# Top-k attention and a PReLU MLP on one core: a hand-written drain with masks on VectorE, and another order on TensorE

## The chip, the cores and the metric

The kernel runs on one core of a Trainium2 chip. The core has five engines that run their own instruction streams: TensorE (PE in the profile; its weight loads are PEld), VectorE (DVE), ScalarE (ACT), GpSimd (POOL) and SyncE (SP, used here to issue DMAs). The metric is the device time of one execution in microseconds (us), and the median over the runs is compared.

## The reference

For 8 batches and 8 heads of 576 tokens with 64 dimensions, attention keeps in each row only the scores that are at least as large as the row's 32nd largest. The heads are then joined to 4608 tokens of 512 columns, which pass an MLP with 2048 hidden units and a leaky activation with a slope for each unit.

```python
scores = (q @ k.transpose(0, 1, 3, 2)) / sqrt(64)
kth    = np.partition(scores, -32, axis=-1)[..., -32:-31]
scores = np.where(scores >= kth, scores, -1e9)
attn   = softmax(scores) @ v                      # 8 x 8 x 576 x 64
x      = attn.transpose(0, 2, 1, 3).reshape(4608, 512)
h      = x @ w_in                                 # 4608 x 2048
g      = np.maximum(h, 0) + alpha * np.minimum(h, 0)
out    = g @ w_out                                # 4608 x 512, float32
```

## The kernel before

**Tiling.** Two heads form a pair `p` (32 pairs, four to a batch). A "duo" is 128 query rows of both heads of one pair (type "n", with the row block `j` from 0 to 3), or the last 64 rows of both heads of two pairs (type "m", the tails). There are `ND` = 144 duos, 18 to a batch. The last batch has its duos ordered by row block, so that each row block becomes a chunk of 128 tokens for the MLP; the batches before it have chunks of 256 tokens, and the tails of two batches share a chunk of 128.

**The life of a duo `d`**, each step in a later slot:
- `st_qk` (TensorE): scores of the duo into one PSUM tile `ps_sc` (pool `ps_s`, one buffer).
- `st_exit` (ScalarE): copy of the scores to `s_sb` in SBUF, 128 x 2 x 576 in float32.
- slot `d` (VectorE, in `dve_slot`): maxima of 8 over six groups of 96 columns for each head; for two duos together `threshold_steps` (`fold`, `negate`, `least`, `turn`) makes from these a first threshold `p9`, which lies near the wanted one.
- slot `d+2`: `st_count` (ScalarE): the sign of (threshold - score) and its sum, so how many scores lie above; `st_y` (GpSimd): score times sign; `row` (VectorE): the 8 largest of that, so the scores next to the threshold.
- slot `2m+4` of a pair of duos: `pick_steps` (VectorE): from the count and these neighbours the exact 32nd largest, kept in `KT` as a multiple of `BIG` = 2^60.
- slot `d+4`: `st_relu` (ScalarE and GpSimd): Relu(KT - BIG * score), which is 0 for the kept scores and huge for the others, is subtracted from the scores.
- slot `d+5`: `st_exp` (ScalarE): Exp of the result to `w` (bfloat16), and a DMA transpose of `w` to `wT`, issued by SP.
- slot `d+7`: `st_av` (TensorE): `wT` times V, whose 65th column is 1 and gives the sum of the row; `norm_a`, `norm_b` (VectorE): reciprocal and product, for two duos together; `st_xT`: a DMA transpose of the finished rows `x` to `xT` on SP.

**The MLP.** When a chunk's `xT` is issued, `mlp_ready` puts its steps into queues: units of h (16 matmuls of 128 columns, or 8 of 256) into `soon`, from which they go to `hq` two slots later, and parts of the output product (one matmul with `w_lin_b` and four with `w_out_b`, four parts for 128 tokens) into `oq`. `h_pe` issues one unit, `h_dve` the Relu of it to `gT` on VectorE, `o_pe` one part, `o_act` the copy of a finished `pz` to `o_sb` on ScalarE, and `o_sp` the store. A part of the next tokens is held back while a finished `pz` has not been copied (`not stores`). The leaky part of the activation is taken out of the sum beforehand: `w_out_b` holds w_out times (1 - alpha), and `w_lin_b` is w_in times (alpha * w_out).

**The order.** All engines' instructions stand in the order in which the program writes them, slot by slot. In a slot `n` the order on TensorE is: one unit of h (or, if there is none, `keep_warm`: four matmuls on zeros, `rest<-idle` in the profile), the transposes that prepare a later pair (`prep`, tile `tps`), the scores of duo `n+1`, the AV of duo `n-7`, one part of the output product, and at the end a second part if more than two are ready, or else `keep_warm`. The tiles of h, of `prep` and of `keep_warm` share two PSUM buffers (`ps_h`). An additional unit of h goes into an even slot when more than 9 units wait (more than 4 from slot 118 on). In the first 17 slots the wide copies of `prep` go to VectorE.

**The end.** The last four duos have shorter lags, and four more slots (144 to 147) run the same loop; for all duos the path is sign, product, maxima, Relu, subtraction, Exp, transpose, AV. Then a loop issues what remains of the MLP.

Of the kernel before, what the change touches and what calls it, by code (L numbers as in the profile page):

```python
# [17 lines left out]
NG = 6  # L18
# [41 lines left out]
def fast_path(tc, q, k, v, moe_w_in, moe_w_out, moe_alpha, out, flag):  # L60
# [27 lines left out]
    with ExitStack() as ctx:  # L88
# [171 lines left out]
        def norm_of(n):  # L260

            m = n - 7 if n < ND + 1 else {ND + 1: ND - 5, ND + 2: ND - 3, ND + 3: ND - 1}.get(n, 0)
            return m if m > 0 and m % 2 else 0
# [49 lines left out]
        def dve_slot(n, f_late):  # L313

            norm = norm_of(n)
            rows = [d for d in duos_at("row", n)]
            picks = [f for m in duos_at("pick", n) for f in pick_steps(m)]
            if on(n):
                s = T["s", n]
                if n % 2 == 0:  # L320
                    T["up", n // 2] = two.tile([128, 4, NG // 2, 8], FP32, name="up", tag="up")
                up = T["up", n // 2]
                for i in range(2):
                    r = 2 * (n % 2) + i
                    for g in range(NG):
                        o = 24 * r + 8 * (g // 2)
                        m = DVE.max(out=(lo if g % 2 else up)[:, r, g // 2, :],
                                    in_=s[:, i, GW * g:GW * g + GW])
                        if g % 2:
                            sm(m, [], [(o, o + 8)])  # L330
                            if picks:
                                picks.pop(0)()
                if n % 2 == 0:
                    h_dve()
                    for d in rows:
                        row(d, 0)
                    if norm:
                        norm_a(norm)
                    for d in rows:
                        row(d, 1)  # L340
                    if norm:
                        norm_b(norm)
                else:
                    fold, negate, least, turn = threshold_steps(n // 2)
                    fold()
                    h_dve()
                    negate()
                    for d in rows:
                        row(d, 0)
                    least()  # L350
                    turn()
                    for d in rows:
                        row(d, 1)
            else:
                if norm:
                    norm_a(norm)
                    norm_b(norm)
                early = picks and duos_at("pick", n)[0] < ND // 2 - 1
                if early:
                    for f in picks:  # L360
                        f()
                if not norm:
                    h_dve()
                for d in rows:
                    row(d, 0)
                    row(d, 1)
                if not early:
                    for f in picks:
                        f()
                if norm:  # L370
                    h_dve()
            if f_late:
                h_pe()
                h_dve()
# [6 lines left out]
        for d in range(ND):  # L381
            last = d - (ND - 4) if d >= ND - 4 else None
            for kind, lag, drain in (("count", 2, (2, 2, 2, 1)), ("relu", 4, (4, 3, 3, 2)),
                                     ("exp", 5, (5, 4, 4, 3)), ("av", 7, (6, 5, 5, 4))):
                at_slot = d + (lag if last is None else drain[last])
                if d < ND - 4:
                    at_slot = min(at_slot, ND + 1)
                stage.setdefault((kind, at_slot), []).append(d)
        for (kind, n), l in list(stage.items()):
            if kind == "count":  # L390
                stage["row", n] = l
        for m in range(ND // 2):
            stage["pick", 2 * m + (4 if m < ND // 2 - 1 else 3)] = [m]
# [28 lines left out]
        def st_exp(n):  # L422
            w = ws[n % 3]
            ACT.activation(w[:, :, 0:S], T.pop(("s", n)), AF.Exp, scale=att_scale)
            wt = three.tile([128, 10, 128], BF16, name="wT", tag="wT")
# [84 lines left out]
        def mlp_ready(xt, rows):  # L510
            ntok = sum(r[1] for r in rows)
            e_n = 512 // ntok
            ch = {"done": 0}
# [15 lines left out]
            for i in range(NFT // e_n):  # L529
                soon.append((now[0] + 2, lambda i=i: unit(i)))  # L530

            def part(t0, a):
                gt = ch["g"]
                if a == 0:
                    ch["z"] = ps_z.tile([128, DMODEL], FP32, name="pz", tag="z")
# [30 lines left out]
        def h_dve():  # L566
            if act:
                ch, f0, e_n, ph = act.pop(0)
                DVE.tensor_scalar(ch["g"][:, f0:f0 + e_n, :], ph, 0.0, None, ALU.max)
# [152 lines left out]
        for n in range(ND + 4):  # L722
            end = n >= ND
# [4 lines left out]
            if end:  # L728
# [349 lines left out]
```

## Time and profile before

| | |
|---|---|
| median of 3 runs | 839.5 us (837.88 to 840.24) |
| the profiled execution | 840.79 us |
| its span, first to last instruction | 839.0 us, mean granted TensorE clock 0.977 |
| busy: TensorE, VectorE, ScalarE, GpSimd | 751.4, 759.2, 763.5, 753.7 us |
| TensorE, warming matmuls (`rest<-idle`) | 62.4 us, 224 matmuls |
| GpSimd's first product `y` and last subtraction | 20.96 us and about 803.4 us |
| last copy of scores begins | 778.7 us |
| last output copy begins | 831.99 us |

A row of the groups names the engine, the operation, the tile written and the tiles read, the shape and the count; then the busy time and the mean time of one in ns, then the idle time of the engine just before these instructions and what ended it. A row of a timeline gives the start, the time, the engine, the operation and, in brackets, the idle time before it. The line of nearly all instructions is that of a helper (`Ordered`, line 32), so that the tile names tell them apart.

### The profile page before, as it was taken

How to read it: one execution, taken by the hardware profiler on the slowest of the kernel's cores; microseconds unless marked ns; L12 is line 12 of the kernel's file. 1: busy time of each engine (PE TensorE's matmuls, PEld its weight loads, DVE VectorE, ACT ScalarE, POOL GpSimd, SP SyncE). 2: the span in 40 equal slices, each digit the busy share in tenths (PEclk: the TensorE clock that was granted, in tenths of full speed). 3: DMA queues.
4: the chain of work that ended last, by engine and by line, in shares of the span. 5: the costliest groups of instructions: out<-in, count | busy, mean ns of one | idle time of the engine just before them, and what ended most of it. 6: DMA issues, size and time to landing. Idle time of an engine off the chain costs nothing.

```text
span 839.0 us, 17803 instructions
## 1 busy us (share of the span) xinstructions
PE 751.4 (90%) x5382; PEld 426.0 (51%) x5382; DVE 759.2 (90%) x3475; ACT 763.5 (91%) x1255; POOL 753.7 (90%) x706
## 2 busy tenths in 40 slices
PE   8878798998989898898989899898989899989696
PEld 5334344555545554455545455555545555456463
DVE  4879977999999999999999999999999999999731
ACT  4789988999999999999999999999999999999820
POOL 1798988999999999999999999999999999999920
PEclk9979899999999999999999999999999999999898
DMA  6599867556656556556656556556666555444441
GB/s 142 157 165 182 157 124 151 92 122 134 118 120 131 109 103 148 107 133 120 128 114 142 112 96 143 107 132 121 131 113 142 120 96 103 88 83 79 81 87 41
DMA packets 344231, 100.19 MB, mean 119 GB/s; under 512 B 338032, under 2 KB 338048, under 8 KB 344128
## 3 DMA queue, kind: packets, MB, share of 16 engines
q1 hardware_dynamic: 341152, 92.13, 55.6%
q0 software_dynamic: 1776, 6.56, 3.2%
q8 instruction: 44, 0.72, 0.3%
q14 instruction: 59, 0.48, 0.2%
q10 hardware_dynamic: 1200, 0.30, 0.2%
HBM read 36.71 MB, written 9.44 MB: 55 GB/s over the span
## 4 chain that ended last, share of the span: by engine, by line
DVE 38%; POOL 19%; ACT 17%; PE 15%; issue 6%; DMA 3%; SPq 0%; ACTq 0%; POOLq 0%
DVE small L32 11%; DVE p L32 10%; POOL y L32 9%; POOL s_sb L32 9%; DVE up L32 7%; DVE gT L32 5%; ACT r L32 5%; ACT sg L32 5%; PE ps_sc L32 4%; ACT s_sb L32 4%; PE pz L32 3%; ACT w L32 3%; PE ph L32 3%; PE rest L32 2%; DMA wT<-w 2%
## 5 line engine op out<-in xcount | busy, mean ns | idle before, releaser
L32 POOL TENSOR_TENSOR y<-s_sb,sg 128x576 f32<-128x576 f32 x288 | 362.1, 1278 | 40.6 <-ACT sg L32 40.0
L32 POOL TENSOR_TENSOR s_sb<-s_sb,r 128x576 f32<-128x576 f32 x288 | 362.3, 1279 | 8.9 <-ACT r L32 8.6
L32 ACT ACTIVATE sg<-s_sb,p 128x576 bf16<-128x576 f32 x288 | 221.4, 773 | 8.0 <-DVE p L32 6.8
L32 DVE MAX8 p<-y 128x8 f32<-128x576 f32 x288 | 215.1, 747 | 8.1 <-POOL y L32 7.6
L32 DVE MAX8 up<-s_sb 128x8 f32<-128x96 f32 x864 | 211.8, 245 | 9.8 <-ACT s_sb L32 9.8
L32 DVE MAX8 small<-s_sb 128x8 f32<-128x96 f32 x864 | 216.1, 250 | 0.0
L32 ACT ACTIVATE r<-s_sb,KZ 128x576 bf16<-128x576 f32 x288 | 206.6, 769 | 0.4 <-DVE KZ L32 0.4
L32 PE MATMUL ps_sc<-qkT 64*128 64x512 f32 (+2 forms) x768 | 184.1, 569 | 18.7 <-ACT s_sb L32 18.6
L32 ACT COPY s_sb<-ps_sc 128x1152 f32<-128x1152 f32 x144 | 159.2, 1105 | 21.8 <-PE ps_sc L32 21.5
L32 ACT ACTIVATE w<-s_sb 128x1152 bf16<-128x1152 f32 x144 | 166.4, 1156 | 5.9 <-POOL s_sb L32 5.8
L32 PE MATMUL ph<-xT,w_in_b 128*128 128x256 bf16 (+1 forms) x1408 | 150.8, 255 | 5.3 <-ACT qkT L32 2.9
L32 PE MATMUL pz<-w_out_b,gT 128*128 128x512 bf16 x576 | 148.8, 381 | 0.3 <-DVE gT L32 0.3
L32 PEld LDWEIGHTS <-w_in_b 128*128 128x128 bf16 x1408 | 119.2, 99 | 48.7 <-issue 12.0
L32 PE MATMUL xo<-v,wT 128*128 128x65 bf16 (+3 forms) x1600 | 127.0, 199 | 11.2 <-DMA wT<-w 11.2
L32 PEld LDWEIGHTS <-wT 128*128 128x128 bf16 (+3 forms) x1600 | 97.9, 100 | 40.3 <-DMA wT<-w 11.8
L32 DVE TENSOR_SCALAR gT<-ph 128x512 bf16<-128x512 f32 x144 | 97.2, 675 | 19.4 <-PE ph L32 19.3
L32 PEld LDWEIGHTS <-gT 128*128 128x128 bf16 x576 | 55.9, 98 | 71.9 <-issue 16.9
L32 PEld LDWEIGHTS ps_sc<-qkT 64*128 64x128 f32 (+1 forms) x768 | 56.0, 170 | 64.4 <-ACT s_sb L32 30.3
L32 PEld LDWEIGHTS ps_sc<-kd,qkT 128*128 128x128 f32 x256 | 38.3, 189 | 97.7 <-issue 95.4
L32 PE MATMUL pz<-w_lin_b,xT 128*128 128x512 bf16 x144 | 55.6, 386 | 16.4 <-ACT o_sb L32 16.3
L32 PE MATMUL rest<-idle 128*128 128x512 bf16 x224 | 62.4, 409 | 8.6 <-DVE gT L32 5.2
L32 PE MATMUL ps_sc<-kd,qkT 128*128 128x128 f32 x256 | 62.8, 327 | 0.0
(57 smaller groups left out, 572.2 us busy)
## 6 DMA issues: line engine op xcount, KB each, us to landing
k_st<-in_k_dram SPq DMA_DIRECT2D x64, 128.0 KB, 2.8
v_st<-in_v_dram SPq DMA_DIRECT2D x64, 128.0 KB, 2.7
q_st<-in_q_dram SPq DMA_DIRECT2D x62, 128.0 KB, 2.8
out_dram<-o_sb SPq DMA_DIRECT2D x31, 256.0 KB, 2.5
w_st<-in_moe_w_out_dram POOLq DMA_DIRECT2D x4, 1024.0 KB, 6.6
wT<-w SPq DMA_TRANSPOSE x144, 3.5
w_in_b<-in_moe_w_in_dram POOLq DMA_DIRECT2D x4, 512.0 KB, 6.5
k_st<-in_k_dram SPq DMA_DIRECT2D x32, 32.0 KB, 2.7
```

The source lines that it names most:

```text
L32: ins = self.tc.keep_in_program_order(f(*a, **kw))
```

## The change

- **Slots 0 to 143.** On TensorE the scores of duo `n+1` and the AV stand first, then h (or `keep_warm`), then `prep`. The AV and the norm of the duos below 13 come a slot later (lag 8). On VectorE the Relu of h (`h_relu`) stands at the end of the slot; the threshold steps, the row maxima and the norm come before it. Units of h may start one slot after their chunk is issued instead of two. An additional unit goes in when more than 7 wait (even slots); from slot 118 on, when more than 3 wait (any slot) or more than 1 (even slots). From slot 118 on the second part of the output product is issued whenever one is ready.
- **First slots.** In slots 0 to 3 the copies of `prep` go to ScalarE.
- **Drain.** The four extra slots are replaced by a list of steps. For duos 140, 142 and 143 (`D-3`, `D-1`, `D`) `st_all` takes the Exp of all scores, before the threshold is known (into the score PSUM tile for even duos, into an SBUF tile for odd ones), and `st_mask` writes (score >= kth) * Exp to `w` on VectorE. Some Relus of h go to ScalarE. `fill(k)` issues k steps of the MLP, a part if one is ready and else a unit of h.
- **Last chunk.** The output product of the last 128 tokens uses a tile of the score pool and is not held back by an uncopied `pz`.

```diff
         def dve_slot(n, f_late):
...
+            turn = None
+            if n % 2:
+                fold, negate, least, turn = threshold_steps(n // 2)
+                fold()
+                negate()
+            for d in rows:
+                row(d, 0)
+            if turn:
+                least()
+                turn()
+            if norm:
+                norm_a(norm)
+            for d in rows:
+                row(d, 1)
+            if norm:
+                norm_b(norm)
+            h_relu()
             if f_late:
                 h_pe()
-                h_dve()
+                h_relu()
...
+            for kind, lag in (("count", 2), ("relu", 4), ("exp", 5), ("av", 8 if d < 13 else 7)):
+                stage.setdefault((kind, d + lag), []).append(d)
...
-                soon.append((now[0] + 2, lambda i=i: unit(i)))
+                soon.append((now[0] + 1, lambda i=i: unit(i)))
...
+                    if ch["last"]:
+                        ch["z"] = ps_s.tile([128, 1536], FP32, name="ps_last", tag="s")[:, 0:DMODEL]
...
-            if ready() and not stores:
+            if ready() and (not stores or oq[0][0]["last"]):
...
-        for n in range(ND + 4):
+        for n in range(ND):
...
-            if not h_pe() and not end:
-                keep_warm()
             wide_copy = n % 2 and (n, "prep") in todo
-            if n > 3:
-                run(n, "prep", 1)
             if n and on(n + 1):
                 st_qk(n + 1)
-            if n < 4:
-                run(n, "prep", 2)
-            if not end:
-                for m in duos_at("av", n):
-                    st_av(m)
-            late = len(hq) > (9 if n < 118 else 4) and n % 2 == 0 or end
+            for m in duos_at("av", n):
+                st_av(m)
+            if not h_pe():
+                keep_warm()
+            run(n, "prep", 2 if n < 4 else 1)
+            near = n > 117
+            late = len(hq) > (1 if near else 7) and (n % 2 == 0 or near and len(hq) > 3)
...
-                if not (end or ready() > 2) or not o_pe():
-                    if not end and not did:
-                        keep_warm()
+            elif not ready() > (0 if near else 2) or not o_pe():
+                if not did:
+                    keep_warm()
...
-                on_dve = short and n > 16 or wide and (n < 17 or n % 2 == 0)
+                on_dve = n > 3 and (short and n > 16 or wide and (n < 17 or n % 2 == 0))
...
+        def picked(m):
+            for f in pick_steps(m):
+                f()
+            kv = T["kv", m] = two.tile([128, 4], FP32, name="kv", tag="kv")
+            DVE.tensor_scalar(kv, KT[:, 4 * m:4 * m + 4], 1.0 / BIG, None, ALU.mult)
+
+        def st_all(d):
+            if d % 2 == 0:
+                e = two_of(ps_s.tile([128, 1536], FP32, name="e_ps", tag="s"), 960, S)
+            else:
+                e = qk_p.tile([128, 2, S], FP32, name="e_sb", tag="qkT")
+            ACT.activation(e, T["s", d], AF.Exp, scale=att_scale)
+            T["e", d] = e
+
+        def st_mask(d):
+            w, e, s_ = ws[d % 3], T.pop(("e", d)), T.pop(("s", d))
+            kv = T["kv", d // 2]
+            for i in range(2):
+                r = 2 * (d % 2) + i
+                DVE.scalar_tensor_tensor(out=w[:, i, 0:S], in0=s_[:, i, :], scalar=kv[:, r:r + 1],
+                                         in1=e[:, i, :], op0=ALU.is_ge, op1=ALU.mult)
+            st_wT(d)
...
+        D = ND - 1
+        now[0] = ND
+        o_sp()
+        st_av(D - 6)
+        h_pe()
+        st_all(D - 3)
+        st_count(D - 1)
+        st_y(D - 1)
+        st_exp(D - 4)
+        st_count(D)
+        st_y(D)
+        o_act()
+        picked(D // 2 - 1)
+        st_mask(D - 3)
+        fill(2)
+        st_av(D - 5)
+        normed(D - 6)
+        row(D - 1, 0)
+        st_relu(D - 2, 0)
+        st_relu(D - 2, 1)
+        row(D - 1, 1)
+        h_relu()
+        now[0] += 1
+        o_act()
+        fill(2)
+        row(D, 0)
+        h_relu(ACT)
+        st_all(D - 1)
+        row(D, 1)
+        picked(D // 2)
+        st_av(D - 4)
+        fill(1)
+        st_mask(D - 1)
+        h_relu(ACT)
+        st_all(D)
+        normed(D - 4)
+        now[0] += 1
+        o_act()
+        o_sp()
+        fill(2)
+        st_mask(D)
+        st_exp(D - 2)
+        st_av(D - 3)
+        fill(1)
+        h_relu(ACT)
+        st_av(D - 2)
+        normed(D - 2)
+        now[0] += 1
+        o_act()
+        o_sp()
+        fill(3)
+        h_relu(ACT)
+        st_av(D - 1)
+        st_av(D)
+        normed(D)
+        fill(2)
+        check_low()
```

After this list a loop issues the rest of the MLP, one part, one Relu of h (VectorE and ScalarE in turn), one output copy and one store in each round.

More of the change, by code (lines that the diff above doesn't have):

```diff
@@ L315, in dve_slot @@
             norm = norm_of(n)
-            rows = [d for d in duos_at("row", n)]
+            rows = duos_at("count", n)
             picks = [f for m in duos_at("pick", n) for f in pick_steps(m)]
[L318 to L333, printed above, removed]
-                    h_dve()
[L335 to L371, printed above, removed]
@@ L512, in mlp_ready @@
             e_n = 512 // ntok
-            ch = {"done": 0}
+            ch = {"done": 0, "last": rows[-1][0] == NTOK - 192}
             pieces = []
@@ new lines, in fast_path @@
+        o_act()
[18 more added lines that the diff above has]
+        check_low()
+        turn = 0
+        while hq or act or soon or oq or stores:
+            now[0] += 1
+            while h_pe(2):
+                pass
+            o_pe()
+            h_relu((DVE, ACT)[turn % 2])
+            turn += 1
+            o_act()
+            o_sp()
+            if not hq and not act:
```

74 lines of the change are left out of this document (38 added, 36 removed).

## The prediction

> **What bounds the kernel now.** I read the busy times of the page first, then the busy time by stage, then the groups, then who waited for whom, and last the timelines of the start and the end and the chain that ended last.
>
> ```profile
> PE 751.4 (90%) x5382; PEld 426.0 (51%) x5382; DVE 759.2 (90%) x3475; ACT 763.5 (91%) x1255; POOL 753.7 (90%) x706
> ```
> ```profile
> core 0 of [0], span 839.0 us
> core 0: us, PE busy (x) PEld busy (x) DVE busy (x) ACT busy (x) POOL busy (x), PEclk, DMA share, GB/s
> 33.00:160.00 127.00, 107.06 (x620) 52.05 (x618) 109.84 (x494) 116.93 (x193) 115.16 (x111) 0.92 0.76 147
> 160.00:646.00 486.00, 447.39 (x3295) 258.04 (x3292) 476.57 (x2218) 480.50 (x787) 478.56 (x434) 1.00 0.61 122
> 646.00:784.00 138.00, 130.21 (x961) 74.60 (x959) 134.04 (x620) 133.39 (x220) 132.48 (x116) 1.00 0.49 96
> 784.00:839.00 55.00, 39.11 (x383) 26.06 (x379) 18.94 (x43) 17.00 (x26) 17.11 (x15) 0.87 0.33 65
> ```
>
> Four engines at 90% is an average. By stage, VectorE, ScalarE and GpSimd stand at 98 to 99% from 160 to 646 us, so reordering buys little there. In 33 to 160 us they lose 10 to 17 us each. From 784 us, when the last score maxima are through, all three are mostly idle and TensorE is busy 39.11 of 55 us. So there are three places to look at: the ramp, the middle, the drain.
>
> ```profile
> L32 POOL TENSOR_TENSOR y<-s_sb,sg 128x576 f32<-128x576 f32 x288 | 362.1, 1278 | 40.6 <-ACT sg L32 40.0
> L32 POOL TENSOR_TENSOR s_sb<-s_sb,r 128x576 f32<-128x576 f32 x288 | 362.3, 1279 | 8.9 <-ACT r L32 8.6
> L32 ACT ACTIVATE sg<-s_sb,p 128x576 bf16<-128x576 f32 x288 | 221.4, 773 | 8.0 <-DVE p L32 6.8
> L32 DVE MAX8 p<-y 128x8 f32<-128x576 f32 x288 | 215.1, 747 | 8.1 <-POOL y L32 7.6
> ...
> L32 DVE TENSOR_SCALAR gT<-ph 128x512 bf16<-128x512 f32 x144 | 97.2, 675 | 19.4 <-PE ph L32 19.3
> ```
>
> GpSimd has four instructions of 1.28 us for each duo, 5.1 us. It needs the sign from ScalarE, which needs the threshold from VectorE, which needs the score copy. A stall anywhere in that ring is read at GpSimd's idle time.
>
> **Start (first copies by ScalarE, scores ahead of the warming matmuls).** The rows are from the timelines of VectorE, TensorE, ScalarE and GpSimd.
>
> ```profile
> 24.19 1.27 DVE L32 COPY qkT<-tps 128x512 f32<-128x512 f32 x2
> ```
> ```profile
> 24.91 3.09 PE L32 MATMUL rest<-idle 128*128 128x512 bf16 x8 [2.39 <-DVE qkT L32]
> ```
> ```profile
> 29.95 1.12 ACT L32 COPY s_sb<-ps_sc 128x1152 f32<-128x1152 f32 x1 [5.62 <-PE ps_sc L32]
> ```
> ```profile
> 32.81 2.52 POOL L32 TENSOR_TENSOR y<-s_sb,sg 128x576 f32<-128x576 f32 x2 [5.11 <-ACT sg L32]
> ```
>
> Read upwards: GpSimd stood 5.11 us for a sign, ScalarE 5.62 us for scores, and TensorE had two groups of warming matmuls (3.09 us) ahead of those scores, which waited 2.39 us for VectorE's copy of a transpose, because both h buffers were full. The change gives those copies to ScalarE, which is idle by then, and puts the scores ahead of the second warming group. The scores come about 2.4 + 3.09/2, or 3.9 us, earlier. ScalarE spends about 1.3 us on two copies ahead of the signs of duo 1, while GpSimd is still at duo 0. I take -3 us; the bounds are 0 (the sign then waits for VectorE) and -4.5.
>
> **Ramp (scores and AV first; AV a slot later for d below 13).** First GpSimd's waits in 33 to 160 us, then rows of TensorE's and ScalarE's timelines.
>
> ```profile
> POOL y L32 <- ACT sg L32: 16.4, 12, 5.1
> ```
> ```profile
> 54.79 1.07 PE L32 MATMUL xo<-v,wT 128*128 128x65 bf16 x10 [3.05 <-DMA wT<-w]
> 55.79 3.60 PE L32 MATMUL rest<-idle 128*128 128x512 bf16 x8
> ```
> ```profile
> 62.17 1.12 ACT L32 COPY s_sb<-ps_sc 128x1152 f32<-128x1152 f32 x1 [3.22 <-PE ps_sc L32]
> ```
>
> The 16.4 us contain the 5.1 of the start, so 11.3 are left. The pattern is in the three rows: an AV waits 3.05 us for its transposed weights, two warming groups follow (3.60 us), and the scores behind them make ScalarE wait 3.22 us. Now the scores stand ahead of AV, of one of the two groups (1.8 us) and of the transposes of the preparation, and AV has one more slot for its transfer. No work is saved; what moves back are h and the preparation, and who waits for those (the relu and the copies, both at the slot's end) does not hold up the ring. VectorE and ScalarE were busy 109.84 and 116.93 of 127 us, so they could give back some 10 us at most. I take about half of 11.3, -5; bounds 0 and -9.
>
> **Middle (relu at the end of VectorE's slot).** GpSimd's waits for the sign in 160 to 784 us, then ScalarE's for the threshold over the whole span.
>
> ```profile
> POOL y L32 <- ACT sg L32: 6.8, 9, 1.9
> ```
> ```profile
> ACT sg L32 <- DVE p L32: 6.8, 12, 1.1
> ```
>
> The threshold of a pair now leaves VectorE one relu (0.675 us) earlier, which covers most of ScalarE's 12 waits for it (0.57 us in the mean). The price is that an h buffer comes free about 1.3 to 2 us later, by the row maxima (0.747 each) and the norm that now precede the relu. TensorE meets that only where a second h or a warming group asks for the buffer in the same slot. I take -3 us, bounds -7 and +4.
>
> **More MLP steps from slot 118.** The warming matmuls in 646 to 784 us, then TensorE by form in 784 to 839 us.
>
> ```profile
> 646.00:784.00 138.00, 8.21 (x32) 1.00 0.49 96
> ```
> ```profile
> L32 PE MATMUL ph<-xT,w_in_b 128*128 128x128 bf16 x237 | 16.6, 228 | 0.0
> L32 PE MATMUL pz<-w_lin_b,xT 128*128 128x512 bf16 x17 | 6.6, 391 | 2.8 <-ACT o_sb L32 2.8
> ```
> At 784 us there remain 237/16, or 15 units of h, and 17 parts of the output product. By the chain of waits:
>
> ```profile
> 803.42 1.17 ACT w L32
> 804.59 0.02 issue
> 804.61 3.76 DMA wT<-w
> ...
> 813.99 1.79 PE ph L32 x32
> 815.77 1.08 PE pz L32 x5
> ...
> 831.99 0.58 ACT o_sb L32
> ```
>
> two units take 1.79 us and one part 1.08. The last three chunks of 128 tokens have to wait for their attention, 12 units and 12 parts; so at most 3 units and 5 parts, 8 us, can go ahead. Room for them is there in 646 to 784 us: 138 - 130.21 = 7.8 us idle and 8.21 of warming. With h a slot earlier, a second h from four waiting units on, and a second part whenever one is ready, I take 6 us as moved. Each unit brings its relu of 0.675 us to a VectorE that is at 97% there: 3 of them cost the ring +2 us. The 6 us count within the drain.
>
> **Drain.** Rows of GpSimd's, TensorE's and SP's timelines, and one stretch by stage.
>
> ```profile
> 790.66 4.98 POOL L32 TENSOR_TENSOR s_sb<-s_sb,r 128x576 f32<-128x576 f32 x4
> ```
> ```profile
> 792.40 1.07 PE L32 MATMUL xo<-v,wT 128*128 128x65 bf16 x10 [5.13 <-DMA wT<-w]
> 793.40 1.89 PE L32 MATMUL ph<-xT,w_in_b 128*128 128x128 bf16 x16
> ```
> ```profile
> 809.92 1.19 SPq L32 DMA_TRANSPOSE xT<-x  x1
> ```
> ```profile
> 790.00:800.00 10.00, 5.53 (x37) 3.67 (x38) 4.01 (x10) 7.11 (x10) 7.23 (x7) 0.50 0.56 107
> ```
>
> For duos 140, 142 and 143 the change drops two relus of ScalarE and two subtractions of GpSimd (1.28 us) each: 6 x 1.28 = 7.7 us leave GpSimd. It puts an Exp of 1.17 us on ScalarE ahead of the threshold, and six masking instructions on VectorE. No row shows that instruction at this size. The nearest are the maximum over 576 elements, 0.747 us, and the relu, 0.675; the far end is GpSimd's two-input form, 1.28; none is free, as 576 elements have to be read. I take 0.72, 4.3 us for six, on a VectorE with 18.94 us of work in 55.
>
> In the new order the mask of 140 is done near 788 us, where its Exp had to wait for two of the subtractions that begin at 790.66. The rows of 143 are done near 792, the masks of 142 and 143 near 794.5 and 796.5, the Exp of 141 near 796.5, since ScalarE has two full Exps, two relus and two output copies before it. Their three weight transposes stand one behind the other on SP's queue, so the last lands near 802 (before: 804.61 + 3.76 = 808.4). AV of 142 and 143 stands behind three MLP steps, so the last x transpose starts near 808 instead of 809.92. Attention ends only some 2 us earlier. The gain lies in TensorE not standing. Before, it did 39.1 us of work in the 47.9 us from 784 to 831.9, and about 2.7 of those were the half clock of 790 to 800 us (a unit of h 1.89 us against 0.9). So 36.4 us were work at full clock and 11.5 lost. After: 36.4 - 6 = 30.4 us of work, and I leave 6.5 lost (waits of AV, of the last x, of the last relu): 36.9 instead of 47.9, -11 us. The last copy and store, 7 us from 831.99 to the end, stay. Bounds: -4 (nothing moved ahead, most of the standing remains) and -16. Where the MLP steps run out, AV's wait of up to 5 us is seen again.
>
> The half clock follows the 5.13 us stand that begins at 787.3. The Trainium skill (TensorE: Matmul & The Clock Gate, "What's actually happening") says that an idle window of about 3.4 us halves the clock and that some 3.4 us of sustained work restore it. The row agrees on the first; on the second it differs, as the half clock lasted 10 us. By the rule, filled gaps mean no half clock.
>
> A rule that speaks against the change: the Trainium skill (SBUF — State Buffer, "Who interferes with whom") has a VectorE instruction with two SBUF inputs and a GpSimd instruction that reads SBUF exclude each other for a whole instruction. The mask of 143 alone has both inputs in SBUF (140 and 142 read the Exp from PSUM). By it the two masks of 143 would each wait for one subtraction of 141, 2.6 us at most, nothing if these are over by 794 as I have them; the sum would be -17.5 at worst instead of -20. No row of this kernel shows the case.
>
> **Sum.** -3 - 5 - 3 + 2 - 11 = -20 us. The profiled execution took 840.8 us (its span 839.0 and 1.8 around it), so it would become 820.8; the median of the runs, 839.5, lies 1.3 below it: 819.5.
>
> **Rivals.** *Only the drain pays.* The ramp's loss is not TensorE's order but three engines at 86 to 92% that wait on each other in turn. For: the middle shows all three full. Against: the scores' waits of 5.62 and 3.22 us have warming matmuls ahead of them. Then 839.5 - 11, about 829.
>
> *The drain changes its wait.* SP's three transposes and the late Exp of 141 leave TensorE standing, and the half clock comes back: the drain gives -4, the rest -9, so 826.5.
>
> *Slower: the late relu holds the h buffer.*
>
> ```profile
> PE rest L32 <- DVE gT L32: 5.2, 10, 0.8
> ```
>
> TensorE already waited 5.2 us for it, ten times. With the buffer free 1.3 to 2 us later, TensorE stands in each slot with a second h, and the next scores stand behind it. Its slack is (7.8 + 8.2) us over the 26 slots of 646 to 784 us, 0.6 a slot; 1.65 - 0.6, about 1 us, in one of four of the 126 slots from 18 on is 31 us, which turns -20 into +11: 850. It decides from 20 us lost, 0.65 us in each such slot. Against: between two score copies ScalarE has two signs (1.55 us) and an Exp (1.17), so scores may be late by over 2 us before anything waits.
>
> *The edits cancel:* copies on ScalarE delay its signs by what the order gains, and the masks take on VectorE what GpSimd saves: 838 to 840.
>
> **How the numbers follow.** Forecast 0.55, only the drain 0.17, a new wait in the drain 0.15, cancel 0.05, slower 0.08. The low end takes the gains at nearly all of their better bounds for start and drain and two thirds for the rest, about -32: 807. Above, the drain's rivals with a little lost in the middle reach 836. A measurement of this kernel tells about 0.3%, 2.5 us, from no change: faster 0.87, same 0.04, slower 0.09.
>
> **What would show it.** Right: GpSimd's 5.11 us wait down to about 2; ScalarE's waits for scores down by half or more; its wait for the threshold mostly gone; under 15 units of h left after the last score maxima; no TensorE gap above 3.4 us and a clock of 1.0 in the drain; some 37 us from there to the last matmul instead of 48. Wrong: longer TensorE waits for gT, less busy vector engines from 160 us on, masks above 1.2 us, or a half clock in the drain.

## The result: slower, 869.9 us against 838.7

The changed kernel takes 869.89 us (median of 4 runs, 868.97 to 877.8) against 838.69 for the kernel before: a ratio of 1.0393, 95% interval 1.0329 to 1.0457. The forecast was 819.5 with a range of 807 to 836. The direction was wrong.

The page of the changed kernel, and its busy time in four stretches (us; then busy time and count of each engine, the granted clock and DMA). The stretches end at about the same slots as those shown of before: slot 24, slot 117, and the end of the score maxima, within two duos.

```profile
span 867.9 us, 17761 instructions
...
PE 761.7 (88%) x5329; PEld 426.9 (49%) x5414; DVE 766.4 (88%) x3472; ACT 768.1 (89%) x1260; POOL 748.3 (86%) x702
```
```profile
core 0: us, PE busy (x) PEld busy (x) DVE busy (x) ACT busy (x) POOL busy (x), PEclk, DMA share, GB/s
33.00:140.00 107.00, 90.33 (x539) 44.61 (x550) 99.50 (x450) 105.41 (x175) 104.36 (x101) 0.95 0.87 166
140.00:657.00 517.00, 463.82 (x3295) 262.16 (x3348) 487.16 (x2233) 484.89 (x790) 480.17 (x434) 0.98 0.58 115
657.00:820.00 163.00, 146.88 (x1052) 82.92 (x1068) 143.69 (x652) 141.64 (x231) 139.40 (x123) 0.98 0.45 88
820.00:868.00 48.00, 32.61 (x309) 21.39 (x310) 16.71 (x36) 15.44 (x26) 10.70 (x11) 0.91 0.35 69
```

GpSimd, ScalarE and VectorE had been at 98 to 99% between the ramp and slot 117. Now they are at 93 to 94%, and in the last batch at 86 to 88%. The work is the same, so the time is waiting; what they waited for is read below. The ramp is better: three engines lost 10 to 17 us there, now they lose 2 to 8.

The clearest measure is when the copy of each duo's scores begins on ScalarE, read from its timeline. How far a kernel is ahead of the kernel before (minus: behind), in us, at duos 24, 117 and 143, and how long it takes from the last copy to the end of its span:

| kernel | median us | at 24 | at 117 | at 143 | then to the end |
|---|---|---|---|---|---|
| before | 838.69 | 0 | 0 | 0 | 60.3 |
| changed | 869.89 | 12.1 | -17.0 | -35.9 | 53.3 |
| e1 Relu early | 874.85 | 8.5 | -23.3 | -42.0 | 52.9 |
| e2 h first | 918.72 | 11.8 | -55.4 | -85.5 | 52.8 |
| e3 both back | 872.25 | 10.3 | -18.8 | -37.6 | 54.9 |
| e4 old step rules | 856.34 | 10.4 | -6.7 | -17.6 | 60.2 |
| e5 both back, old rules | 831.08 | 9.7 | 8.5 | 8.5 | 60.2 |
| e6 Relu early, old rules | 862.27 | 12.2 | -11.3 | -17.0 | 62.2 |
| e7 h first, old rules | 878.04 | 11.6 | -25.1 | -38.0 | 61.1 |
| e8 = e5, h one slot earlier | 841.43 | 11.8 | 10.5 | 5.2 | 63.9 |
| e9 = e5, second h from 7 | 842.53 | 12.2 | 1.9 | -1.2 | 60.6 |
| e10 = e5, more steps from slot 118 | 834.13 | 9.9 | 8.8 | 2.7 | 57.6 |
| e11 = e5, drain in another order | 827.06 | 9.6 | 8.7 | 8.7 | 54.4 |
| e12 = e4, parts ready a slot later | 839.55 | 8.3 | 0.0 | -5.3 | 61.9 |
| e13 = e4, preparation first | 859.36 | 11.7 | -9.8 | -21.5 | 60.5 |
| e14 = e4, both of these | 838.70 | 10.8 | 8.0 | 3.9 | 61.0 |

The profiled execution of e12 took 847.9 us, 8 above its median, so its row of differences is worse than its usual run; that of e8 lies 2 us below its median. Kernels that are alike up to slot 18 differ there by up to 2 us, so smaller differences in the table are not read.

So the changed kernel gains 12 us by slot 24, loses 29 from 24 to 117 and 19 from 117 to 143, and gains 7 behind that: 12.1 - 29.1 - 18.9 + 7.0 = -28.9, the difference of the spans (839.0 and 867.9).

**Start and ramp.** GpSimd's first wait that was 5.11 us, and its waits up to slot 24, which were 11.3 us besides:

```profile
29.49 2.51 POOL L32 TENSOR_TENSOR y<-s_sb,sg 128x576 f32<-128x576 f32 x2 [1.85 <-ACT sg L32]
```
```profile
POOL y L32 <- ACT sg L32: 2.3, 5, 0.8
```

**The middle.** TensorE's timeline in the changed kernel, one slot, and then ScalarE's and VectorE's next instruction that waited for it:

```profile
428.58 1.05 PE L32 MATMUL ph<-xT,w_in_b 128*128 128x256 bf16 x8
429.46 0.38 PE L32 MATMUL pz<-w_lin_b,xT 128*128 128x512 bf16 x1
429.68 0.59 PE L32 MATMUL pz<-w_out_b,gT 128*128 128x512 bf16 x2
432.79 1.03 PE L32 MATMUL pz<-w_out_b,gT 128*128 128x512 bf16 x2 [2.52 <-DVE gT L32]
433.75 2.08 PE L32 MATMUL ps_sc<-qkT 64*128 64x512 f32 x4
```
```profile
436.54 1.12 ACT L32 COPY s_sb<-ps_sc 128x1152 f32<-128x1152 f32 x1 [0.54 <-PE ps_sc L32]
```
```profile
437.10 0.18 DVE L32 RECIPROCAL KZ<-xo 128x4 f32<-128x4 f32 x1 [1.50 <-PE xo L32]
```

The unit of h ends at 429.6. A part of the output product is issued behind it whose last two matmuls need the Relu of that unit. The Relu stands at the end of VectorE's slot and runs at 432.06. TensorE stands 2.52 us in the middle of a part, the next scores and AV stand behind it, and ScalarE and VectorE then wait for those. The stand costs more than its own time: TensorE's granted clock (the third figure from the right) is then halved for 3.41 us, and the four score matmuls take 2.08 us, against 1.13 in the slots before. Two stretches, in the columns of the table above:

```profile
429.39:432.80 3.41, 0.89 (x7) 0.27 (x5) 3.34 (x15) 3.24 (x6) 3.41 (x4) 1.00 0.75 152
432.80:436.21 3.41, 3.41 (x8) 1.07 (x9) 2.81 (x16) 3.20 (x6) 3.41 (x4) 0.50 0.38 78
```

Not every stand is followed by this: the trace of the changed kernel has five such stretches of half clock between slots 24 and 117, that of the kernel before none.

The program allowed the part that stood because `ready()` counts a Relu as done when it is written, not when it has run; while the Relu came early in VectorE's slot, that made no difference. The other pattern is on VectorE, where a second unit of h ends a slot:

```profile
416.18 0.69 DVE L32 TENSOR_SCALAR gT<-ph 128x512 bf16<-128x512 f32 x1 [1.13 <-PE ph L32]
```
```profile
421.41 0.78 ACT L32 ACTIVATE sg<-s_sb,p 128x576 bf16<-128x576 f32 x1 [1.70 <-DVE p L32]
```
```profile
422.36 2.51 POOL L32 TENSOR_TENSOR y<-s_sb,sg 128x576 f32<-128x576 f32 x2 [1.47 <-ACT sg L32]
```

VectorE stands 1.13 us for h and is late with the next threshold, and the wait runs through ScalarE to GpSimd. In 160 to 640 us, GpSimd's waits for the sign, at the end of these chains, and TensorE's waits of parts for the Relu, each before and then after; the last row, of after alone, is a wait of the warming matmuls for ScalarE's copies:

```profile
POOL y L32 <- ACT sg L32: 3.4, 4, 1.9
PE pz L32 <- DVE gT L32: 0.3, 1, 0.3
```
```profile
POOL y L32 <- ACT sg L32: 24.7, 19, 3.2
PE pz L32 <- DVE gT L32: 16.5, 9, 2.9
PE rest L32 <- ACT qkT L32: 8.1, 7, 1.8
```

### The profile page after: what moved, and what is told of

The parts are those of the page before. It is cut to its first block, busy times and chain, and to the rows that moved or that the text cites. A ratio compares the mean times of both kernels' runs of the same rounds, so it can differ in the third digit from the quotient of the medians.

```text
span 867.9 us, 17761 instructions
## 1 busy us (share of the span) xinstructions
PE 761.7 (88%) x5329; PEld 426.9 (49%) x5414; DVE 766.4 (88%) x3472; ACT 768.1 (89%) x1260; POOL 748.3 (86%) x702
## 4 chain that ended last, share of the span: by engine, by line
DVE 40%; PE 30%; POOL 12%; ACT 9%; issue 4%; DMA 3%; SPq 1%; ACTq 0%; POOLq 0%; DVEq 0%
DVE small L32 11%; DVE p L32 10%; PE ps_sc L32 9%; PE pz L32 7%; DVE up L32 7%; PE ph L32 6%; POOL y L32 6%; DVE gT L32 5%; POOL s_sb L32 5%; PE xo L32 5%; ACT sg L32 3%; ACT r L32 2%; ACT s_sb L32 2%; DVE qkT L32 2%; DMA wT<-w 2%
## 5 line engine op out<-in xcount | busy, mean ns | idle before, releaser
L32 POOL TENSOR_TENSOR s_sb<-s_sb,r 128x576 f32<-128x576 f32 x282 | 354.6, 1279 | 14.6 <-ACT r L32 14.3
L32 ACT ACTIVATE sg<-s_sb,p 128x576 bf16<-128x576 f32 x288 | 221.3, 773 | 16.8 <-DVE p L32 16.0
L32 ACT ACTIVATE r<-s_sb,KZ 128x576 bf16<-128x576 f32 x282 | 202.4, 768 | 2.9 <-DVE KZ L32 2.9
L32 PE MATMUL pz<-w_out_b,gT 128*128 128x512 bf16 x539 | 146.7, 388 | 24.4 <-DVE gT L32 20.1
L32 PE MATMUL ph<-xT,w_in_b 128*128 128x256 bf16 (+1 forms) x1408 | 153.7, 257 | 13.7 <-DVE gT L32 7.7
L32 ACT ACTIVATE w<-s_sb 128x1152 bf16<-128x1152 f32 x141 | 162.8, 1155 | 1.8 <-POOL s_sb L32 1.6
L32 PEld LDWEIGHTS <-w_in_b 128*128 128x128 bf16 x1408 | 111.3, 99 | 33.7 <-issue 11.3
L32 DVE TENSOR_SCALAR gT<-ph 128x512 bf16<-128x512 f32 x137 | 92.9, 679 | 26.1 <-PE ph L32 26.0
L32 PEld LDWEIGHTS ps_sc<-qkT 64*128 64x128 f32 (+1 forms) x768 | 53.3, 170 | 117.4 <-ACT s_sb L32 56.4
L32 PEld LDWEIGHTS ps_sc<-kd,qkT 128*128 128x128 f32 x256 | 39.1, 193 | 100.7 <-issue 94.7
L32 PE MATMUL rest<-idle 128*128 128x512 bf16 x234 | 66.5, 394 | 16.1 <-ACT qkT L32 9.6
L32 ACT ACTIVATION_READ_ACCUMULATOR sg<-s_sb,p 128x1 f32 x288 | 55.8, 194 | 0.0
```

The lines of the kernel that those rows point to most:

```text
L32: ins = self.tc.keep_in_program_order(f(*a, **kw))
```

## The experiments

Three theories: RELU, the late Relu; ORDER, h and preparation behind scores and AV; STEPS, the rules for additional MLP steps. Rows of waits below give the sum, the number and the longest, over slots 24 to 117 unless stated.

**e1, e2 and e3: the order and the Relu undone, with the new step rules.**

```diff
# e1, in dve_slot
                 fold()
+                h_relu()
                 negate()
+            else:                # even slots, after the maxima
+                h_relu()
...
                 norm_b(norm)
-            h_relu()
# e2, slots from 24 on
+                if not h_pe():
+                    keep_warm()
+                run(n, "prep", 1)
             if n and on(n + 1):
                 st_qk(n + 1)
             for m in duos_at("av", n):
                 st_av(m)
-            if not h_pe():
-                keep_warm()
-            run(n, "prep", 2 if n < 4 else 1)
# e3: both, from slot 24 on
```

> The changed kernel with one thing undone: the Relu of h stands again where it stood before in VectorE's slot (after the maxima in even slots, after the fold in odd ones). Before and after, the copies of the scores stand apart by -12 us at slot 24 (the changed kernel ahead), +17 at slot 117, +34 at slot 141. Theory RELU (the late Relu makes the parts of the output product wait for gT, with the next scores behind them): most of the 29 us of slots 24 to 117 come back, TensorE's 16.5 us of waits for gT in 160 to 650 us vanish, time 835 to 845. Rival ORDER (h behind scores and AV is what is late; an early Relu then waits on VectorE for h): no gain or a loss, 870 to 900, with VectorE's waits for h at over 60 us.

> The changed kernel with h (or the warming matmuls) and the preparation ahead of scores and AV again from slot 24 on; the Relu of h stays at the slot's end. ORDER: the 29 us of slots 24 to 117 come back, 840 or less. RELU: the parts still wait for the Relu at the slot's end; at most a third comes back, 860 or more. STEPS (more units and parts overfill TensorE): no change, about 870.

> The changed kernel with both undone from slot 24 on: Relu early and h first; start, ramp, additional MLP steps and drain stay as changed. If RELU and ORDER together hold the loss of slots 24 to 117: 12 us ahead at slot 24, still 10 to 12 ahead at slot 117. If the additional steps cost nothing themselves, the drain's 6 us come on top: about 820. STEPS as the cause of the 17 us of slots 118 to 143: 835 to 840.

874.85, 918.72 and 872.25 us (ratios 1.044, 1.0961 and 1.0399; intervals 1.0416 to 1.0464, 1.0935 to 1.0986, 1.0375 to 1.0424). None recovers anything. e1 came out as ORDER had it, e2 against it and 49 us above the changed kernel, which no theory had said, and e3 far above the 840 that any theory allowed. With the Relu early, VectorE waits for h, at half of the size that ORDER gave (e1):

```profile
DVE gT L32 <- PE ph L32: 30.7, 40, 3.6
```

With both back, another wait shows: h is issued before its transposed x has landed, with the scores behind it (e3).

```profile
PE ph L32 <- DMA xT<-x: 16.5, 6, 5.0
```

So e3 was not the undoing that I took it for: with h first, the new rule "one slot after the chunk" seems to have a price of its own. It leaves the step rules as the thing to take away first.

**e4: only the step rules undone.**

```diff
-                soon.append((now[0] + 1, lambda i=i: unit(i)))
+                soon.append((now[0] + 2, lambda i=i: unit(i)))
-            late = len(hq) > (1 if near else 7) and (n % 2 == 0 or near and len(hq) > 3)
+            late = len(hq) > (9 if n < 118 else 4) and n % 2 == 0
-            elif not ready() > (0 if near else 2) or not o_pe():
+            elif not ready() > 2 or not o_pe():
```

> The changed kernel with the old rules for MLP steps: a second unit of h only when more than 9 wait (4 from slot 118), a second part only when more than two are ready, h two slots after its chunk. STEPS: slots 118 to 143 lose nothing, and fewer second units in the middle: 840 to 850. RELU and ORDER: the middle still loses over 20 us; 860 to 870, as what the last batch gains is done in the drain.

856.34 us (1.0207, 1.0174 to 1.0239): 13.6 of the 31 us come back. The loss between slots 24 and 117 falls from 29 to 17 us and that up to 143 from 19 to 11, while the tail is 7 us longer. The time lies between the two forecasts: STEPS is right in part, and order and Relu still lose 28 us from slot 24 to 143 under the old rules.

**e5, e6 and e7: the other three combinations of order and Relu under the old step rules.** The diffs are those of e3, e1 (from slot 24) and e2, each with that of e4.

> From slot 24 on everything as before: h first, Relu early, the old rules for MLP steps (9 and 4 waiting, more than two ready parts, h two slots after its chunk). Of the change remain the start, the ramp and the drain. SUM (the losses all lie in the order and the step rules, and the gains of start, ramp and drain are separate from them): the copies of the scores stay 10 to 12 us ahead from slot 24 to 143, the drain gives 5 or more: 818 to 825. Rival KNOT (the middle is an equilibrium that falls back to its own pace, and what the ramp gains is lost by slot 143 anyway): 830 to 838.

> Scores and AV first as changed, but the Relu early from slot 24 on, and the old rules for MLP steps. RELU: with the step rules out of the way the late Relu is what is left of the loss: 840 or less, no waits of TensorE for gT. ORDER: VectorE waits for h in its slot and the threshold is late: 855 to 870.

> h first as before from slot 24 on, the Relu at the slot's end as changed, old rules for MLP steps. With e4, e5 and e6 the four combinations of order and Relu under the old step rules. RELU: the late Relu alone costs 20 us or more against e5 (840 or above), TensorE's next warming matmuls, preparation or parts wait for gT. ORDER: within 5 us of e5.

831.08 us (0.9892, 0.9859 to 0.9925), 862.27 (1.0295, 1.0236 to 1.0353) and 878.04 (1.0447, 1.0407 to 1.0486). In e5 the lead stays at 8.4 to 8.7 us from slot 30 to 143: the middle has the old pace and the ramp's gain is kept. The time lies in KNOT's range, but KNOT's reason, a gain lost by slot 143, falls. e5 is 1.1% faster than the kernel before. SUM's reason holds and its 818 to 825 does not, because I counted a lead of 10 to 12 us and 5 for the drain; the drain takes 60.2 us, as before. e6 (862.27, where ORDER had it) and e7 (878.04, where RELU had it) show that each half of the reordering alone is worse than both (e4). e6, VectorE and ScalarE (in e5 these waits were 1.1 and 2.7 us):

```profile
DVE gT L32 <- PE ph L32: 23.4, 41, 1.3
```
```profile
ACT sg L32 <- DVE p L32: 25.3, 30, 1.7
```

e7, TensorE:

```profile
PE ph L32 <- DVE gT L32: 20.7, 29, 1.1
PE pz L32 <- DVE gT L32: 15.6, 11, 1.8
PE tps L32 <- DVE gT L32: 11.2, 16, 2.1
```

With scores first and the Relu early, VectorE asks for an h that is not there. With h first and the Relu late, TensorE asks for buffers and Relus that are not there, ahead of the scores. RELU and ORDER are not two causes that add up: the two places belong together.

Nor do the order and the step rules add up. The step rules alone, on the old order (e3 against e5), cost 41.2 us; order and Relu alone, under the old rules (e4 against e5), 25.3; both together, the changed kernel, 38.8. Each of the two is enough to make the kernel slower, and undoing one alone cannot show the whole of the other.

**e8, e9 and e10: the step rules one at a time on e5.**

```diff
# e8
-                soon.append((now[0] + 2, lambda i=i: unit(i)))
+                soon.append((now[0] + 1, lambda i=i: unit(i)))
# e9
-            late = len(hq) > (9 if n < 118 else 4) and n % 2 == 0
+            late = len(hq) > (7 if n < 118 else 4) and n % 2 == 0
# e10
-            late = len(hq) > (9 if n < 118 else 4) and n % 2 == 0
+            late = len(hq) > (1 if near else 9) and (n % 2 == 0 or near and len(hq) > 3)
-            elif not ready() > 2 or not o_pe():
+            elif not ready() > (0 if near else 2) or not o_pe():
```

> e5 with one rule of the change put back: h one slot after its chunk is issued instead of two. In e3, with all three step rules of the change, TensorE waited 16.5 us in 160 to 640 us for the transposed x (6 times, 5.0 us at the longest) with the scores behind it. SOON (that rule alone is the step rules' loss in the middle): 20 us or more above e5. Rival SECOND (the second units of h from 7 waiting are): within 5 us of e5.

> e5 with one rule of the change put back: a second unit of h in even slots below 118 when more than 7 wait, instead of 9. e8 lost nothing up to slot 132, so if the step rules hold the middle's loss in e3 (30 us between slots 24 and 117), it is this one alone: SECOND says 15 us or more above e5, lost evenly between slots 24 and 117. Rival PAIR (only with h one slot after its chunk, when a unit is issued before its x has landed, does it cost): within 3 us of e5.

> e5 with the change's rules from slot 118 on put back: a second unit of h from more than 3 waiting (1 in even slots) and a second part whenever one is ready. STEPS: slots 118 to 143 lose 8 us or more and the drain gives back up to 6, as fewer units remain: 833 to 840. Rival FREE (the steps use idle TensorE time, and the loss there in the changed kernel came from its order): no loss in the slots, 822 to 826.

841.43 us (1.0023, 1.0007 to 1.0039), 842.53 (1.0038, 1.0021 to 1.0056) and 834.13 (0.9941, 0.9923 to 0.9959): 10.4, 11.5 and 3.1 above e5. e8 lies between the forecasts of SOON and SECOND. It loses nothing up to slot 132; behind it one wait for x is most of the 5.3 us that the lead loses there (TensorE, 629 to 774 us), and its tail is 3.6 us longer:

```profile
PE ph L32 <- DMA xT<-x: 4.6, 1, 4.6
```

e9 loses 10 us between slots 24 and 117, below the 15 that SECOND asked for, but spread over the middle and with only 1.7 us of waits for x, so PAIR's "within 3 us" falls. GpSimd's waits there, which were 4.7 us in e5:

```profile
POOL y L32 <- ACT sg L32: 11.5, 9, 2.6
```

Something of PAIR stands all the same. Up to slot 117 e3 is e5 with the rules of e8 and e9 together; it loses 29 us between slots 24 and 117, where e8 alone loses 1 and e9 alone 10. By which wait the second unit costs e9 its 10 us, no run separates.

In e10 the slots from 118 on lose 6.1 us and the tail gives back 2.6: STEPS in the sign, at three quarters of its size, with a time in its range.

**e11: e5 with another order in the drain.**

```diff
         picked(D // 2 - 1)
+        normed(D - 6)
+        h_relu()
         st_mask(D - 3)
         fill(2)
+        o_act()
         st_av(D - 5)
-        normed(D - 6)
...
+        st_exp(D - 2)
+        h_relu()
         st_mask(D)
-        st_exp(D - 2)
...
```

and the `fill` calls moved and issue two steps more in all, and there is one more `o_sp` (a step of stores).

> e5 with its drain written in another order. In e5 the same 39.2 us of TensorE work as before lie in the drain, and TensorE stood 2.7 us for the norm of 137 behind the mask of 140, 4.1 us for the weight transpose of 141 that SP took up behind the one of 143, and ran at half clock for 10 us. Here the norm of 137 stands ahead of the mask of 140, the Exp of 141 and its transpose ahead of the mask of 143, one output copy earlier, and two more MLP steps and two more Relus in between. STAND (these waits and the half clock are why the drain did not shorten): 4 to 8 us less than e5, 823 to 827. Rival BACKLOG (the tail is bound by TensorE's work alone): within 2 us of e5.

827.06 us (0.984, 0.9799 to 0.9882): 4.0 below e5, and from the last score copy to the end 54.4 instead of 60.2 us. STAND is right, at the weak end of its range, and BACKLOG falls. In e5 TensorE had:

```profile
780.87 0.78 PE L32 MATMUL xo<-v,wT 128*128 128x65 bf16 x10 [2.67 <-DVE x L32]
...
794.33 1.07 PE L32 MATMUL xo<-v,wT 128*128 128x65 bf16 x10 [4.12 <-DMA wT<-w]
```
and in e11:
```profile
779.01 0.78 PE L32 MATMUL xo<-v,wT 128*128 128x65 bf16 x10 [1.01 <-DVE x L32]
...
793.23 0.79 PE L32 MATMUL xo<-v,wT 128*128 128x65 bf16 x10 [2.95 <-DMA wT<-w]
```

The two stands are 2.8 us shorter, and the half clock of e5's drain is gone (the last section has its rows). Which of the edits brought how much was not separated. e11 is 1.6% faster than the kernel before.

**e12, e13 and e14: by which wait the order loses under the old step rules.**

```diff
# e12, in h_relu, for the slots 0 to 143
-                ch["done"] += e_n
+                fresh.append((ch, e_n))
# and at the start of the next slot
+                ch["done"] += e_n
# e13, slots from 24 on
+                run(n, "prep", 1)
             if n and on(n + 1):
                 st_qk(n + 1)
# and no longer behind h; e14: both
```

> e4 (order and late Relu as changed, old step rules) with one thing changed: a part of the output product counts as ready only from the slot after the Relu of its h, so that no part is issued in the slot whose end it would have to wait for. e4 loses 15 us from slot 24 to 117 and 13 from 118 to 143. PARTS (TensorE's 18.9 us of waits of parts for gT, with the next scores behind them, are the loss): these waits nearly vanish, 8 us or more of the 15 come back, 845 or less. PREP (the late preparation, whose copies ScalarE then waits for and which holds an h buffer, is the loss): less than 4 us come back, above 852.

> e4 with the transposes of the preparation ahead of scores and AV again from slot 24 on (h stays behind them, the Relu stays late). PREP: ScalarE's wait for the transposes (5.4 us) and the warming matmuls' for ScalarE's copies (12.8 us) vanish, 8 us or more of the 15 come back, 845 or less. PARTS: less than 4, above 852.

> e4 with both: parts ready a slot later and the preparation first. If the two hold all of what the order costs under the old step rules, the copies of the scores stay 8 to 12 us ahead to slot 117: 835 or less. If h behind the scores itself is a cost (VectorE at the slot's end waits for h, 4.1 us in e4), 840 to 850.

839.55 us (0.9984, 0.9964 to 1.0004), 859.36 (1.0209, 1.0155 to 1.0262) and 838.7 (0.9986, 0.997 to 1.0002). PARTS is shown for the order under the old step rules: one rule, a part is not issued in the slot whose end it would wait for, brings back 16.8 of the 25.3 us between e4 and e5. In the changed kernel itself, with the new step rules, this was not tried. TensorE's row of e4 that has gone from e12:

```profile
PE pz L32 <- DVE gT L32: 18.9, 11, 2.9
```

PREP alone brings nothing: in e13 parts still wait 18.5 us for the Relu, and the transposes, now ahead of the scores, wait 12.9 us for it themselves. e14 keeps its 8.0 us up to slot 117, as far as its forecast of 8 to 12 goes, but at 838.7 it stays above the 835 and below the 840 of the other forecast, and no faster than e12 beyond the noise. Of the 7.6 us by which it stands above e5, some 4 lie between slots 117 and 143; by which wait is open.

## Why the prediction was wrong, step by step

**Start, -3:** right, -3.0 at the seventh copy, by the mechanism that was named. **Ramp, -5:** right. It measured -9 at slot 24, its better bound, but that point lies high: e5, whose middle has the old pace, keeps 8.5 us of both, so 5.5 of the ramp.

**Middle, -3 with bounds -7 and +4: this step failed, +29 up to slot 117 and +19 more up to 143, together with the step rules.** The sentence that failed stands in the step on the ramp: "who waits for those (the relu and the copies, both at the slot's end) does not hold up the ring". VectorE's Relu of h and the copies of the preparation run on the ring's own engines, so an engine of the ring that waits for a late h is the ring waiting. And I looked for the price of the late Relu only at the h buffers. The buffers do cost something (7.7 us of waits of h for the Relu over the whole run), but the larger wait is that of a part for the Relu's data, 20.1 us, which a count in the program lets through. And the half clock that follows such a stand was looked for in the drain only. The 29 us cannot be split between the order and the step rules: the reordering alone loses 17 us between slots 24 and 117 and 11 up to 143 (e4), the step rules alone 29 and 19 (e3), both together 29 and 19.

**More MLP steps, +2, 6 us moved:** the moved work was sized right, the price was not. TensorE's busy time behind the last maxima fell from 39.1 to 32.6 us. TensorE by form behind the last maxima, in the changed kernel (820 to 868 us) and in e5 (775.5 to 831):

```profile
L32 PE MATMUL ph<-xT,w_in_b 128*128 128x128 bf16 x176 | 12.7, 229 | 2.1 <-DMA xT<-x 1.7 <-DVE lo L32 0.4
```
```profile
L32 PE MATMUL ph<-xT,w_in_b 128*128 128x128 bf16 x238 | 16.2, 224 | 0.4 <-DVE lo L32 0.4
```

176/16 is 11 units, where 15 remained before: 4 moved, one more than I had thought could. The price was not +2 but 6 us (e10, which moved 3 units) in the slots from 118 on, for 2.6 in the tail. The second units before slot 118 (e9, 10 us) and h a slot earlier (e8, 5 us in the slots and 4 in the tail), which I had costed at nothing, came on top, and together they cost more (e3). I had taken idle time of TensorE in a stage for room; that the cost comes from Relus that fall due on a full engine fits these runs, but no run shows it by itself.

**Drain, -11: failed, 0 by itself.** The terms that I had from rows held: the masks took 0.81 us in the mean against 0.72, no more with both inputs in SBUF than with one in PSUM:

```profile
L32 DVE SCALAR_TENSOR_TENSOR w<-s_sb,kv,e_ps 128x576 bf16<-128x576 f32 x4 | 3.1, 812 | 1.8 <-ACT e_ps L32 1.7
...
L32 DVE SCALAR_TENSOR_TENSOR w<-s_sb,kv,e_sb 128x576 bf16<-128x576 f32 x2 | 1.5, 814 | 0.4 <-ACT e_sb L32 0.4
```

As the subtractions of 141 were over before the masks of 143, no run shows what the two would do together, and the rule of the Trainium skill (SBUF — State Buffer, "Who interferes with whom") that such instructions exclude each other is not tried. What failed is "I leave 6.5 lost", and with it "Attention ends only some 2 us earlier": in e5 the last transpose of `x` starts 30.9 us after the last copy of scores, against 31.2 before. In e5, with the same work left as before, TensorE lost as much as before, at new places: the norm of 137 now behind a mask, the transposes of the weights in SP's order, and the half clock that followed. The 7.0 us of the changed kernel's tail go with the work that was moved into slots where it cost more: the four kernels with the new step rules (changed, e1, e2, e3) have tails of 52.8 to 54.9 us, the four with the same drain and the old rules (e4 to e7) 60.2 to 62.2.

**The rivals.** "Slower: the late relu holds the h buffer" had the right engine and the right consequence (TensorE stands, the next scores stand behind it), the smaller of the waits, and a third of the loss (+11 us against +31), at 0.08. I had argued against it that scores may be late by over 2 us. The stands were up to 2.9 us, and came on top of TensorE's own lag. "The drain changes its wait" (0.15) had the drain right in kind: SP's order of transposes left TensorE standing and the half clock came back, though the drain then gave nothing where the rival kept 4 us. Three of the four signs of being wrong came: longer waits for gT, vector engines less busy from 160 us on, and a half clock in the drain.

## What to carry to other kernels

Where a program issues work by its own count of what is ready, moving the producer later in its slot turns that count into a stall: move the count with it. In a schedule in which three engines are 98% full, a consumer and its producer on another engine have to be moved together; here each of the two moves alone cost 31 to 47 us against e5, both together 25. Idle time of an engine in a stage is not a budget: steps moved into it in e9 and e10 cost 10 and 6 us in stages where TensorE had idle time and the engine that takes its output had almost none.

## What the runs showed of the hardware

The half clock of TensorE comes after shorter stands than I had read from the kernel before, and not always. The granted clock (the third figure from the right) in e5's drain, then in e11's:

```profile
core 0: us, PE busy (x) PEld busy (x) DVE busy (x) ACT busy (x) POOL busy (x), PEclk, DMA share, GB/s
775.00:781.50 6.50, 3.78 (x51) 2.88 (x48) 6.22 (x18) 6.50 (x13) 6.44 (x6) 1.00 0.58 92
781.50:785.00 3.50, 2.82 (x9) 1.15 (x9) 3.31 (x9) 3.50 (x6) 3.50 (x4) 0.53 0.58 110
785.00:791.80 6.80, 5.05 (x61) 3.63 (x59) 3.50 (x6) 2.17 (x3) 0.33 (x1) 0.99 0.65 144
791.80:798.60 6.80, 3.93 (x25) 2.58 (x27) 0.61 (x2) 0.59 (x1) 0.00 (x0) 0.51 0.32 61
```
```profile
781.50:785.00 3.50, 3.50 (x32) 2.08 (x31) 3.31 (x9) 1.59 (x2) 3.50 (x4) 1.00 0.51 96
785.00:791.80 6.80, 5.12 (x74) 4.21 (x72) 4.20 (x7) 4.28 (x6) 0.94 (x3) 1.00 0.83 128
791.80:798.60 6.80, 5.32 (x56) 3.60 (x58) 0.65 (x3) 0.00 (x0) 0.26 (x1) 1.00 0.68 116
```

In e5 a stand of 2.67 us was followed by a stretch of some 3.5 us at half clock, and one of 4.12 us by some 6.8; in e11 a stand of 2.95 us by none. The Trainium skill (TensorE: Matmul & The Clock Gate, "What's actually happening") gives one idle window of about 3.4 us as the condition and calls the window free-running. The lengths are about one and two such windows. That a stand below 3.4 us can halve the clock differs from the page's figure.

How a stand falls into the windows decides in these traces. Within each of the sixteen traces of this case all changes of the granted clock lie on one grid of 3.41 us. On that grid, the window that holds e5's shorter stand and the one behind it, then the two windows over which e11's stand spreads:

```profile
778.29:781.70 3.41, 0.78 (x10) 0.65 (x11) 3.27 (x7) 3.41 (x7) 3.35 (x4) 1.00 0.49 91
781.70:785.11 3.41, 2.78 (x7) 1.02 (x7) 3.22 (x9) 3.41 (x6) 3.41 (x4) 0.50 0.53 101
```
```profile
788.75:792.17 3.42, 1.53 (x28) 1.35 (x25) 1.21 (x2) 1.57 (x3) 1.08 (x2) 1.00 1.28 150
792.17:795.58 3.41, 2.29 (x17) 1.33 (x19) 0.61 (x2) 0.00 (x0) 0.00 (x0) 1.00 1.13 187
```

e5's 2.67 us lie, but for 0.1 us, in one window and leave TensorE 0.78 us of work in it; e11's 2.95 us are cut in two and leave 1.53 and 2.29. Over the sixteen traces, from 50 us after the start to the last matmul, a window at full clock in which TensorE had no matmul for more than 2.0 us was followed by a window at half clock in 50 of 50 cases, with less than 1.4 us in 3 of 3358, and in between in 51 of 150.
